# Strassen's seven products in the output stage of a sparse-attention and bilinear feed-forward kernel

## The chip, the cores and the metric

The kernel runs on one core of a Trainium2 chip. The metric is the device time of one execution in microseconds (us), lower is better. Before the change the median was 344.7 us of three runs. An executed program has a span in the profile, from its first to its last instruction, that is about 2 us shorter than the time of the same run. Tile lengths and waits below are parts of a span.

The engines are TensorE (PE; weight loads are PEld), VectorE (DVE), ScalarE (ACT), GpSimd (POOL) and SyncE (SP, whose queue issues transfers and is listed as SPq).

## The reference, cut to what matters

```python
def _attn_ref(q, k, v):                       # 8 batches, 8 heads, 576 tokens, 64 per head
    scores = scale * np.matmul(q, k.transpose(0, 1, 3, 2))
    # heads 0..3: a causal window of 32;  heads 4..7: causal, every 32nd token
    scores = np.where(masks[None], scores, -1e9)
    attn = softmax(scores)                    # written out in the original
    return np.matmul(attn, v)

def _moe_ref(x, w_a, w_b, w_out):             # x: 4608 x 512, w_a and w_b: 512 x 1536, w_out: 1536 x 512
    return (x @ w_a) * (x @ w_b) @ w_out
```

## The kernel before

The 4608 tokens are nine tiles of 512. A tile has 16 slots on TensorE: twelve for the products a and b (one slice of 128 of the 1536 inner columns each, 8 matmuls of 512 columns), then four for the output (12 matmuls each). The attention of the next batches is woven in between the slots. ScalarE copies a out of PSUM, VectorE multiplies it by b, and the product `pf` goes into SBUF as bf16:

```python
def ffn_ab(t, f, mid, ab=None):
    ...
    ab_mm(t, f, ab, range(KD), mid)                       # 2 x 4 matmuls 128x128 by 128x512
    nc.scalar.copy(a_sb, ab[0])
    nc.vector.tensor_mul(pf[:, f, :], a_sb, ab[1])

def ffn_y(t, j, mid):                                     # 128 of the 512 tokens
    ...
        y = psum4["mm"].tile([128, n], F32, ...)          # n = 512 but for the last group
        for f in range(FD):                               # FD = 12
            nc.tensor.matmul(y, lhsT=pf[:, f, 128 * j:128 * (j + 1)], rhs=wo_sb[:, f, c0:c0 + n], ...)
        (nc.scalar.copy if act else nc.vector.tensor_copy)(y_sb, y)
        (nc.scalar if z == 2 else nc.sync).dma_start(out=out[r0:r0 + 128, c0:c0 + n], in_=y_sb)
```

The store is four transfers of 256 KB per tile, whose first dimension is 128 rows of the output. From batch 2 on, the queries and keys of the next batch are transposed by VectorE (`step_D`), and pieces of the result are copied from SBUF to SBUF into `qz` and `kT`, in which the score matmuls (`st`) read them. These copies use the same queue as the stores, SyncE's:

```python
def step_D(b, z, nm, part):
    nc.vector.transpose(t..., src...)
    if last:
        ...
            for e in range(2):                            # both for k and for q
                nc.sync.dma_start(out=dst..., in_=t[64 * c:64 * c + 64, e])            # kT
                for j in range(2):
                    nc.sync.dma_start(out=qz_buf[b % 2][j][z]..., in_=t[r0:r0 + 32, e])  # qz
```

The softmax here doesn't subtract the row's maximum and nothing guards it: scores larger than these inputs give would overflow.

## Time and profile before

| | before |
|---|---|
| time, median of 4 runs | 344.25 us (343.21 to 344.76) |
| span of the profiled run | 341.5 us |
| TensorE busy | 98% of the span |
| granted clock | full in all slices |
| tiles 2, 3, 4, 5 | 35.92, 35.46, 35.45, 35.45 us |
| tiles 6, 7, 8 (to the end of PE) | 34.70, 31.08, 31.30 us |
| after the last matmul | 3.45 us |

Tile lengths are read as the distance from the first a/b matmul of one tile to that of the next. The busy times by stretches are shown in the prediction below. The first is of the kernel before, the stores by their line (columns: line, queue, kind, destination and source, count: shortest, median, longest time to issue one in ns, first and last start).

```profile
L554 SPq DMA_DIRECT2D out_dram<-y_sb x37: 332/338/527, 48.8 to 337.8; - x37
...
DMA to landing us min/median/max: 1.6/2.2/5.9
```

At the median a store of 256 KB holds the queue for 0.34 us. The second is the order of time on SyncE's queue, at the start of tile 3 (start, duration, queue, line, what, count).

```profile
132.41 3.13 SPq L554 DMA_DIRECT2D out_dram<-y_sb  x2
140.98 0.55 SPq L302 DMA_DIRECT2D qz00s<-tq  x1
141.58 0.58 SPq L302 DMA_DIRECT2D qz01s<-tq  x1
```

The last two stores of tile 2 (a row that names several issues spans from the first to the end of the last, with gaps) are out at 135.5 us. VectorE has transposed q at 141; the copies of q follow without a gap, about 0.6 us each. The fourth of these copies is in the chain of waits, with the time from its issue to its landing:

```profile
142.84 3.64 DMA qz01s<-tq
```

The score matmuls start as it lands, at 146.52, so this time has little slack. Even so, in the view of waits, all that TensorE waited for copies of q over the span is three waits of 1.2, 0.7 and 0.5 us.

### The profile page before, as it was taken

What the parts mean: (1) busy time and instruction counts of PE and PEld (TensorE: products, weight loads), DVE (VectorE), ACT (ScalarE), POOL (GpSimd) and SP (SyncE); (2) the same over time, 40 slices, a digit from 0 to 9 for tenths busy, and PEclk for the clock granted to TensorE, in tenths of its full rate; (3) what the DMA queues carried; (4) which work ended last, traced back from release to release, by engine and by line L of the source; (5) the groups of instructions that cost most, each with busy time, mean ns of one, the idle gap of its engine ahead of it and who ended that gap; (6) DMA issues with size and microseconds to landing.
All of it is one profiled execution on the core that took longest, in us unless ns stands there. A gap on an engine that the chain in (4) does not pass through costs nothing.

```text
span 341.5 us, 6887 instructions
## 1 busy us (share of the span) xinstructions
PE 333.1 (98%) x2520; PEld 173.7 (51%) x2520; DVE 205.1 (60%) x400; ACT 203.9 (60%) x331; POOL 140.4 (41%) x247
## 2 busy tenths in 40 slices
PE   8999999989989999999999999999999999999995
PEld 6754555445545555555555555555555444444444
DVE  6866657758759766876578846885666333303331
ACT  5754865368767765876587657775688533223311
POOL 8945539898537434653465346633000000000000
PEclk9999999999999999999999999999999999999999
DMA  9999999997999599969997989888220110021002
GB/s 160 154 203 197 202 176 172 179 154 89 129 200 101 90 99 185 99 110 91 165 104 133 77 168 96 132 80 145 76 59 2 61 63 0 0 92 34 0 31 94
DMA packets 102242, 37.56 MB, mean 110 GB/s; under 512 B 77632, under 2 KB 97728, under 8 KB 102208
## 3 DMA queue, kind: packets, MB, share of 16 engines
q0 software_dynamic: 87760, 19.58, 63.7%
q1 hardware_dynamic: 14304, 17.47, 16.2%
q8 instruction: 20, 0.33, 0.4%
q14 instruction: 14, 0.11, 0.1%
q10 hardware_dynamic: 144, 0.07, 0.1%
HBM read 39.71 MB, written 9.44 MB: 144 GB/s over the span
## 4 chain that ended last, share of the span: by engine, by line
PE 70%; DMA 17%; SPq 3%; DVE 3%; ACT 3%; POOL 2%; issue 2%; DVEq 0%; ACTq 0%
PE mm L518 41%; PE mm L546 20%; DMA vl<-in_v_dram 4%; PE o L438 3%; PE st L340 3%; DMA k<-in_k_dram 3%; DMA wa_sb<-in_moe_w_a_dram 3%; SPq L302 2%; DMA qz01l<-tq 2%; PE misc L153 2%; DMA out_dram<-y_sb 1%; DMA qz01s<-tq 1%; ACT xr L447 1%; DMA qz11s<-tq 1%; DVE tq L283 1%
## 5 line engine op out<-in xcount | busy, mean ns | idle before, releaser
L518 PE MATMUL mm<-xT,wb_sb 128*128 128x512 bf16 x424 | 110.1, 379 | 0.3
L518 PE MATMUL mm<-xT,wa_sb 128*128 128x512 bf16 x424 | 110.2, 379 | 0.1
L536 DVE TENSOR_TENSOR pf<-a_sb,mm 128x512 bf16<-128x512 f32 x106 | 71.9, 678 | 48.3 <-PE mm L518 25.5
L546 PE MATMUL mm<-wo_sb,pf 128*128 128x512 bf16 (+2 forms) x456 | 99.6, 368 | 0.1
L535 ACT COPY a_sb<-mm 128x512 f32<-128x512 f32 x106 | 62.1, 586 | 45.4 <-PE mm L518 43.0
L518 PEld LDWEIGHTS <-wb_sb 128*128 128x128 bf16 x432 | 41.7, 98 | 49.5 <-issue 1.3
L546 PEld LDWEIGHTS <-pf 128*128 128x128 bf16 x456 | 41.5, 98 | 42.3 <-issue 0.4
L518 PEld LDWEIGHTS <-wa_sb 128*128 128x128 bf16 x432 | 38.1, 98 | 34.2 <-issue 0.2
L552 ACT COPY y_sb<-mm 128x512 f32<-128x512 f32 (+2 forms) x35 | 20.0, 571 | 46.6 <-PE mm L546 38.6
L348 ACT ACTIVATE p<-st 128x576 bf16<-128x576 f32 (+1 forms) x64 | 41.7, 651 | 8.8 <-PE st L340 8.2
L447 ACT ACTIVATE xr<-o 64x576 f32<-64x576 f32 x48 | 31.1, 647 | 23.5 <-PE o L438 23.3
L454 DVE TENSOR_TENSOR xT<-o,xr 64x288 bf16<-64x288 f32 x48 | 21.6, 450 | 33.1 <-ACT xr L448 32.8
L448 ACT ACTIVATE xr<-xr 64x576 f32<-64x576 f32 x48 | 32.8, 682 | 1.5
L452 DVE TENSOR_TENSOR xT<-o,xr 64x288 bf16<-64x288 f32 x48 | 21.6, 450 | 16.9 <-ACT xr L448 16.4
L678 POOL CAST pace<-pf 1x1 f32<-1x1 bf16 x51 | 11.6, 227 | 41.5 <-DVE pf L536 41.3
L358 DVE TENSOR_TENSOR p<-p,mask_l 128x576 int16<-128x576 int16 x32 | 14.6, 455 | 17.1 <-ACT p L348 17.1
L218 POOL DMA_DIRECT2D vs<-in_v_dram x24 | 19.6, 817 | 9.9 <-issue 9.9
L194 POOL DMA_DIRECT2D kl<-in_k_dram x24 | 16.0, 666 | 6.7 <-issue 5.0
L194 POOL DMA_DIRECT2D ql<-in_q_dram x24 | 16.0, 666 | 6.6 <-DMA wo_sb<-in_moe_w_out_dram 3.8
L185 POOL DMA_DIRECT2D natk<-in_k_dram x24 | 14.6, 610 | 3.6 <-issue 3.0
L185 POOL DMA_DIRECT2D natq<-in_q_dram x24 | 14.6, 609 | 0.0
L678 POOL COPY pace<-y_sb 1x1 f32<-1x1 f32 x22 | 4.2, 189 | 24.2 <-ACT y_sb L552 24.2
(116 smaller groups left out, 316.2 us busy)
## 6 DMA issues: line engine op xcount, KB each, us to landing
out_dram<-y_sb SPq DMA_DIRECT2D x35, 256.0 KB, 2.4
vl<-in_v_dram POOLq DMA_DIRECT2D x7, 384.0 KB, 6.6
kl<-in_k_dram POOLq DMA_DIRECT2D x24, 72.0 KB, 2.8
ql<-in_q_dram POOLq DMA_DIRECT2D x24, 72.0 KB, 3.3
vs<-in_v_dram POOLq DMA_DIRECT2D x24, 72.0 KB, 3.6
wo_sb<-in_moe_w_out_dram POOLq DMA_DIRECT2D x4, 384.0 KB, 11.9
natk<-in_k_dram POOLq DMA_DIRECT2D x20, 72.0 KB, 3.3
natq<-in_q_dram POOLq DMA_DIRECT2D x20, 72.0 KB, 3.3
```

The lines of the kernel that those rows point to most:

```text
L185: nc.gpsimd.dma_start(out=t[32 * h:32 * h + n], in_=bass.AP(tensor=src.tensor, offset=(b * H + HL + h) * S * D, ap=[[RS * D, n], [YS * RS ...
L194: nc.gpsimd.dma_start(out=t[32 * h:32 * h + 32], in_=src[b, h].rearrange("(i y) d -> y i d", y=32))
L348: nc.scalar.activation(p[:M, :, :W], st[:M, :, :W], ACT.Exp, scale=scale)
L447: nc.scalar.activation(r, sums, ACT.Ln)
L448: nc.scalar.activation(r, r, ACT.Exp, scale=-1.0)
L452: nc.vector.tensor_mul(dst[:, W * half:W * (half + 1)], o[:64, j, :W], r[:, j])
L454: nc.vector.tensor_mul(dst.rearrange("d (p r) -> d p r", r=RS)[:, :, G * half:G * (half + 1)], o[:64, j, :W].rearrange("d (g p) -> d p g", ...
L518: nc.tensor.matmul(ps_, lhsT=w[:, kk, 128 * f:128 * (f + 1)], rhs=xT[:, kk, TTOK * t:TTOK * (t + 1)], start=(kk == first), stop=(kk == last))
L535: nc.scalar.copy(a_sb, ab[0])
L536: nc.vector.tensor_mul(pf[:, f, :], a_sb, ab[1])
L546: nc.tensor.matmul(y, lhsT=pf[:, f, 128 * j:128 * (j + 1)], rhs=wo_sb[:, f, c0:c0 + n], start=(f == 0), stop=(f == FD - 1))
L552: (nc.scalar.copy if act else nc.vector.tensor_copy)(y_sb, y)
```

## The change

An output tile is seen as a 2 by 2 block product: the tokens in two halves, the inner dimension in even and odd slices, the output columns in two halves of 256. Strassen's scheme, in the form with few additions, makes this from seven products in place of eight. TensorE is what the kernel is bound by, so one eighth of the output matmuls is to be saved, at the price of additions on engines that have time.

- TensorE: 84 matmuls of 256 columns per tile in place of 48 of 512, for tiles 2 to 8, in an order of products that frees banks early ("3417526", in the last tile "3412567").
- VectorE: nine sums of `pf` per tile, ten sums of the weights once (in the slots of tile 2), four additions that read PSUM.
- GpSimd: the last two subtractions per tile.
- ScalarE: three copies out of PSUM in place of four.
- The tokens of one half aren't neighbours. They alternate with the other half in runs of 16, so `pf` is written in that order, and the store is taken apart again: eight stores of 128 KB per tile, each of which writes 8 runs of 16 rows.
- Room for this: xT holds four batches in place of eight (which cuts tile 4's matmuls in two halves), some loads share a buffer with the sums, and a fourth bank joins the rotation of `mm`.

```diff
@@ ffn_ab @@
-        nc.vector.tensor_mul(pf[:, f, :], a_sb, ab[1])
+        if t in FAST_Y:                                    # tiles 2 to 8
+            halves = lambda x: x.rearrange("p (a i s) -> p a i s", i=2, s=16)
+            nc.vector.tensor_mul(pf[:, f, :].rearrange("p (i a s) -> p a i s", i=2, s=16), halves(a_sb), halves(ab[1]))
+        else: ...
@@ the sums @@
+    def fast_w(n, gs):   # five sums of quarters of the weights, two pieces each
+        nc.vector.tensor_tensor(wf[:, n, gs], a[:, gs], b[:, gs], op=op)
+    def fast_s(t, n, gs):   # sums of quarters of pf
+        if n == 0:   nc.vector.tensor_tensor(s[:, :, 0:HT], x[:, :, 0, 0], x[:, :, 1, 1], op=ALU.add)
+        elif n == 1: ...                                   # 1024 elements
+        else: ...                                          # 1024 elements
@@ the output, y_plan @@
+        def store(y, i, j, q=slice(0, 2), n=slice(0, HN)):
+            rows = out[TTOK * t:TTOK * (t + 1), HN * j:HN * (j + 1)].rearrange("(q a i s) c -> a s i q c", q=2, i=2, s=16)
+            for z in range(q.start, q.stop):
+                nc.sync.dma_start(out=rows[:, :, i, z, n], in_=y[:, z, n])
+        def post(k): ...                 # what follows each product; among others:
+                    nc.gpsimd.tensor_tensor(v["y11"], v["e"], v["y12"], op=ALU.subtract)
+                    store(v["y11"], 0, 0)
+        for k in "3412567" if tail else "3417526":
+            ...
+                    for g in range(FG):                    # 6
+                        nc.tensor.matmul(dst, lhsT=lhs(g, q), rhs=rhs(g)[:, n], ...)
@@ the schedule @@
+        for n in range(5):
+            for z in range(2):
+                do(32 + 2 * n + z, fast_w, n, slice(3 * z, 3 * z + 3))      # slots of tile 2
+        for t in FAST_Y: ...             # fast_s in slots 3 to 11 of each tile
```

Cut: the ring of xT, the shared buffer, `mm_bank`, most of `post`, and the special last product of tile 8.

More of the change, by code (lines that the diff above doesn't have):

```diff
@@ L26 @@
 WCH = (0, 2, 5, 8, 10, 12)
+FAST_Y = (2, 3, 4, 5, 6, 7, 8)
 @with_exitstack
@@ L156 @@
     cur = {}
-    xT = const.tile([128, KD, n_tok], BF16)
+    XR = 4
+    xT = const.tile([128, KD, XR * S], BF16)
     wa_sb = wp.tile([128, KD, d_ff], BF16)
@@ L160 @@
     wo_sb = wp.tile([128, FD, d_model], BF16)
+    FG = FD // 2
+    HT = TTOK // 2
+    HN = d_model // 2
+    wf = wp.tile([128, 5, FG, HN], BF16, name="wf")
+    wov = wo_sb.rearrange("p (g e) (j n) -> p e j g n", e=2, j=2)
+    def fast_w(n, gs):
+        a, b, op = ((wov[:, 0, 1], wov[:, 1, 1], ALU.subtract), (wov[:, 1, 0], wov[:, 0, 0], ALU.subtract),
+                    (wov[:, 0, 0], wov[:, 1, 1], ALU.add), (wov[:, 0, 0], wov[:, 0, 1], ALU.add),
+                    (wov[:, 1, 0], wov[:, 1, 1], ALU.add))[n]
+        nc.vector.tensor_tensor(wf[:, n, gs], a[:, gs], b[:, gs], op=op)
     tl = {}
@@ L168 @@
     nats = {}
+    shared = {}
     def load_qk(b, strided, heads=range(HL), names="kq"):
@@ L174, in load_qk @@
                 n, R, h0 = (NP, RS, HL) if strided else (96, RL, 0)
-                if (b, nm, strided) not in nats:
-                    nats[b, nm, strided] = nat.tile([n, HL, R, D], BF16, tag=f"{nm}{R}", name=f"{nm}{R}", bufs=1)
-                t = nats[b, nm, strided]
+                w0 = {"k6": 0, "q6": 1536, "k8": 3072, "q8": 5120}[f"{nm}{R}"]
+                if b not in shared:
+                    shared[b] = nat.tile([128, 5 * FD * TTOK // 4], BF16, tag="shared", name="shared")
+                t = nats[b, nm, strided] = shared[b][:n, w0:w0 + HL * R * D].rearrange("p (h r d) -> p h r d", r=R, d=D)
                 hs = slice(heads[0], heads[-1] + 1)
@@ L449, in step_VT @@
         for j in range(2):
-            dst = xT[64 * j:64 * j + 64, c, S * b:S * (b + 1)]
+            dst = xT[64 * j:64 * j + 64, c, S * (b % XR):S * (b % XR + 1)]
             if c < 2:
@@ L469, in X_e @@
         tv = tp.rearrange("d (g p) -> d g p", p=n)
-        dst = xT[:, c, S * b:S * (b + 1)]
+        dst = xT[:, c, S * (b % XR):S * (b % XR + 1)]
         if c >= 2:
@@ L511, with mm_bank @@
     pfs = {}
+    used = [0]
+    def mm_bank(shape):
+        nm = "tp" if used[0] % 4 == 3 and used[0] >= 0 else "mm"
+        used[0] += 1
+        return psum4[nm].tile(shape, F32, tag=nm, name="mm")
     def ab_mm(t, f, ab, kks, mid=None, first=0, last=KD - 1):
+        n = min(TTOK, XR * S - TTOK * t % (XR * S))
+        cuts = [(0, n)] + ([(n, TTOK - n)] if n < TTOK else [])
         for w, ps_ in zip((wa_sb, wb_sb), ab):
@@ L517, in ab_mm @@
             for kk in kks:
-                nc.tensor.matmul(ps_, lhsT=w[:, kk, 128 * f:128 * (f + 1)], rhs=xT[:, kk, TTOK * t:TTOK * (t + 1)],
-                                 start=(kk == first), stop=(kk == last))
+                for c0, n in cuts:
+                    x0 = (TTOK * t + c0) % (XR * S)
+                    nc.tensor.matmul(ps_[:, c0:c0 + n], lhsT=w[:, kk, 128 * f:128 * (f + 1)], rhs=xT[:, kk, x0:x0 + n],
+                                     start=(kk == first and c0 == 0), stop=(kk == last and c0 == cuts[-1][0]))
     def ffn_ab(t, f, mid, ab=None):
@@ L525, in ffn_ab @@
         if ab is None:
-            ab = [psum4["mm"].tile([128, TTOK], F32, tag="mm", name="mm") for _ in range(2)]
+            ab = [mm_bank([128, TTOK]) for _ in range(2)]
             if f == 0:
@@ L535, in ffn_ab @@
         nc.scalar.copy(a_sb, ab[0])
-        nc.vector.tensor_mul(pf[:, f, :], a_sb, ab[1])
-        return pf[:1, f, :1]
+        if t in FAST_Y:
+            halves = lambda x: x.rearrange("p (a i s) -> p a i s", i=2, s=16)
+            nc.vector.tensor_mul(pf[:, f, :].rearrange("p (i a s) -> p a i s", i=2, s=16), halves(a_sb), halves(ab[1]))
+        else:
+            nc.vector.tensor_mul(pf[:, f, :], a_sb, ab[1])
+        return pf[:1, f, :1]
+    pss = {}
+    def fast_s(t, n, gs):
+        if t not in pss:
+            pss[t] = nat.tile([128, 5 * FD * TTOK // 4], BF16, tag="shared", name="ps").rearrange("p (g m) -> p g m", g=FG)
+        s = pss[t][:, gs]
+        x = pfs[t].rearrange("p (g e) (i m) -> p g e i m", e=2, i=2)[:, gs]
+        if n == 0:
+            nc.vector.tensor_tensor(s[:, :, 0:HT], x[:, :, 0, 0], x[:, :, 1, 1], op=ALU.add)
+        elif n == 1:
+            nc.vector.tensor_tensor(s[:, :, HT:3 * HT].rearrange("p g (i m) -> p g i m", i=2), x[:, :, 0], x[:, :, 1], op=ALU.add)
+        else:
+            nc.vector.tensor_tensor(s[:, :, 3 * HT:].rearrange("p g (e m) -> p g e m", e=2), x[:, :, :, 1], x[:, :, :, 0],
+                                    op=ALU.subtract)
@@ new lines, with y_plan, f32t, post @@
+    yst = {}
+    def y_plan(t):
+        pf, s = pfs[t], pss[t]
+        full = lambda e, i: (lambda g, q: pf[:, 2 * g + e, HT * i + 128 * q:HT * i + 128 * (q + 1)])
+        summed = lambda n: (lambda g, q: s[:, g, HT * n + 128 * q:HT * n + 128 * (q + 1)])
+        wsum = lambda n: (lambda g: wf[:, n, g])
+        wfull = lambda e, j: (lambda g: wov[:, e, j, g])
+        bank = {}
+        v = {}
+        def f32t(nm, bufs):
+            return fsb.tile([128, 2, HN], F32, tag=nm, name=nm, bufs=bufs)
+        def store(y, i, j, q=slice(0, 2), n=slice(0, HN)):
+            rows = out[TTOK * t:TTOK * (t + 1), HN * j:HN * (j + 1)].rearrange("(q a i s) c -> a s i q c", q=2, i=2, s=16)
+            for z in range(q.start, q.stop):
+                nc.sync.dma_start(out=rows[:, :, i, z, n], in_=y[:, z, n])
+        def post(k):
+            if k == "3":
+                v["a"] = f32t("ya", 1)
+                nc.scalar.copy(v["a"], bank["a"])
+            elif k == "4":
+                v["w"] = v["a"]
+                nc.vector.tensor_tensor(v["w"], bank["b"], v["a"], op=ALU.add)
+            elif k == "1":
+                v["e"] = f32t("ye", 1)
+                nc.vector.tensor_tensor(v["e"], bank["c"], v["w"], op=ALU.add)
+            elif k == "7":
+                nc.vector.tensor_tensor(v["e"], v["e"], bank["d"], op=ALU.subtract)
+            elif k == "2":
+                v["y21"] = f32t("y_sb", 4)
+                nc.scalar.copy(v["y21"], bank["b"])
+                store(v["y21"], 1, 0)
+                if tail:
+                    nc.gpsimd.tensor_tensor(v["w"], v["w"], v["y21"], op=ALU.subtract)
+            elif k == "5":
+                v["y12"] = f32t("y_sb", 4)
+                nc.scalar.copy(v["y12"], bank["a"])
+                store(v["y12"], 0, 1)
+                if tail:
+                    nc.gpsimd.tensor_tensor(v["e"], v["e"], v["y12"], op=ALU.subtract)
+                else:
+                    v["y11"] = f32t("y_sb", 4)
+                    nc.gpsimd.tensor_tensor(v["y11"], v["e"], v["y12"], op=ALU.subtract)
+                    store(v["y11"], 0, 0)
+            else:
+                v["y22"] = f32t("y_sb", 4)
+                if tail:
+                    nc.vector.tensor_tensor(v["y22"], bank["c"], v["w"], op=ALU.add)
+                else:
+                    nc.vector.tensor_tensor(v["w"], bank["c"], v["w"], op=ALU.add)
+                    nc.gpsimd.tensor_tensor(v["y22"], v["w"], v["y21"], op=ALU.subtract)
+                store(v["y22"], 1, 1)
+        def y11(d, q=slice(0, 2), n=slice(0, HN)):
+            if "y11" not in v:
+                v["y11"] = f32t("y_sb", 4)
+            nc.vector.tensor_tensor(v["y11"][:, q, n], v["e"][:, q, n], d, op=ALU.subtract)
+            store(v["y11"], 0, 0, q, n)
+        tail = t == NT - 1
+        plan = {"3": ("a", full(0, 0), wsum(0)), "4": ("b", full(1, 1), wsum(1)), "1": ("c", summed(0), wsum(2)),
+                "2": ("b", summed(2), wfull(0, 0)), "5": ("a", summed(1), wfull(1, 1)), "6": ("c", summed(3), wsum(3)),
+                "7": ("d", summed(4), wsum(4))}
+        for k in "3412567" if tail else "3417526":
+            b, lhs, rhs = plan[k]
+            new = b not in bank
+            if new and not (tail and k == "7"):
+                bank[b] = mm_bank([128, 2, HN])
+            for q in range(2):
+                cuts = (slice(0, HN),)
+                if tail and k == "7":
+                    if q == 1:
+                        cuts = (slice(0, 128), slice(128, HN))
+                        end = psum4["o"].tile([128, 2, 512], F32, tag="o", name="end")
+                    else:
+                        end = mm_bank([128, 1, 512])
+                for z, n in enumerate(cuts):
+                    dst = end[:, z, :n.stop - n.start] if tail and k == "7" else bank[b][:, q, n]
+                    for g in range(FG):
+                        nc.tensor.matmul(dst, lhsT=lhs(g, q), rhs=rhs(g)[:, n], start=g == 0 and (tail and k == "7" or new and q == 0),
+                                         stop=g == FG - 1, skip_group_check=True)
+                        if g == FG - 1:
+                            if tail and k == "7":
+                                y11(dst.unsqueeze(1), slice(q, q + 1), n)
+                            elif q == 1:
+                                post(k)
+                        yield v
@@ L539, in ffn_y, with ffn_ys @@
+    def ffn_ys(t, j, mid):
+        if j == 0:
+            yst[t] = y_plan(t)
+        n = 21 + (6 if (t, j) == (NT - 1, 3) else 0)
+        for i in range(n):
+            v = next(yst[t])
+            if i == n // 2:
+                mid()
+        if j == 3:
+            for _ in yst[t]:
+                pass
+        return v[("a", "e", "e", "w")[j]][:1, 0, :1]
     def ffn_y(t, j, mid):
@@ L543, in ffn_y @@
         for z, n in enumerate((256, 128, 128) if (t, j) == (NT - 1, 3) else (d_model,)):
-            y = psum4["mm"].tile([128, n], F32, tag="mm", name="mm")
+            y = mm_bank([128, n])
             for f in range(FD):
@@ L549, in ffn_y @@
                     mid()
-            y_sb = fsb.tile([128, n], F32, tag="y_sb", name="y_sb", bufs=3)
+            y_sb = fsb.tile([128, n], F32, tag="y_sb", name="y_sb", bufs=4)
             act = t < NT - 1 or (j + z) % 2 == 1
@@ L631 @@
         for t in range(NT):
-            slots += [(ffn_ab, t, f) for f in range(FD)] + [(ffn_y, t, j) for j in range(4)]
+            slots += [(ffn_ab, t, f) for f in range(FD)] + [(ffn_ys if t in FAST_Y else ffn_y, t, j) for j in range(4)]
         steps = {}
@@ L672 @@
             do(i, fill_v, t)
+        for n in range(5):
+            for z in range(2):
+                do(32 + 2 * n + z, fast_w, n, slice(3 * z, 3 * z + 3))
+        for t in FAST_Y:
+            for n, at_ in ((0, (3, 7, 11)), (2, (4, 8, 11)), (1, (5, 9, 11))):
+                for z in range(3):
+                    do(16 * t + at_[z], fast_s, t, n, slice(2 * z, 2 * z + 2))
         for i, (fn, t, j) in enumerate(slots):
+            if i == 0:
+                used[0] = -1000 * 3
+            elif i == 16:
+                used[0] = 0
             mid = lambda: take(i - 0.5)
-            done = fn(t, j, mid) if fn is ffn_y else fn(t, j, mid, first.get(j) if t == 0 else None)
+            done = fn(t, j, mid) if fn is not ffn_ab else fn(t, j, mid, first.get(j) if t == 0 else None)
             if i > 13 and i in at:
```

## The prediction

> **What bounds the kernel now.** I read the page first (busy shares, the chain that ended last), then busy time by stretches cut at the token tiles, then the groups of instructions, then the order of time around one tile and around the end. The page's first part:
>
> ```profile
> PE 333.1 (98%) x2520; PEld 173.7 (51%) x2520; DVE 205.1 (60%) x400; ACT 203.9 (60%) x331; POOL 140.4 (41%) x247
> ```
>
> TensorE is busy in 98% of the span, at full granted clock in every slice, and the chain that ended last is 70% TensorE, 41% of it the a/b products and 20% the output products (the line that the change rewrites). Busy time by stretches shows that this holds within each tile (columns: window, length, then busy us and instructions of each engine, clock, DMA share, GB/s). The windows are tiles 2, 3, 4, 5, 6, 7 and 8:
>
> ```profile
> 98.60:134.50 35.90, 35.74 (x260) 18.27 (x258) 26.65 (x49) 25.01 (x41) 18.07 (x35) 1.00 0.91 127
> 134.50:170.00 35.50, 35.42 (x262) 18.32 (x259) 24.79 (x46) 24.91 (x40) 17.94 (x35) 1.00 0.91 119
> 170.00:205.50 35.50, 35.47 (x262) 18.29 (x259) 24.80 (x46) 24.91 (x40) 18.01 (x35) 1.00 0.92 119
> 205.50:241.00 35.50, 35.46 (x262) 18.34 (x259) 24.80 (x46) 24.96 (x41) 16.58 (x33) 1.00 0.92 119
> 241.00:275.80 34.80, 34.80 (x249) 17.76 (x246) 19.24 (x37) 24.32 (x39) 0.44 (x2) 1.00 0.14 45
> 275.80:306.90 31.10, 31.10 (x146) 14.07 (x144) 8.25 (x12) 9.38 (x16) 0.00 (x0) 1.00 0.09 34
> 306.90:338.00 31.10, 31.10 (x169) 15.33 (x166) 9.92 (x15) 8.58 (x15) 0.00 (x0) 1.00 0.10 35
> ```
>
> The reader should see two things: PE (first pair) fills every one of these tiles, so a matmul less is time less; and VectorE (third pair) has 24.8 of 35.5 us in tiles 3 to 5, 26.65 in tile 2, but 8 to 10 in tiles 7 and 8. So the room for more VectorE work is about 10 us in an attention tile and 20 us after the attention.
>
> **What one output matmul costs, and one of half its width.** The mean durations in the groups (379 ns for 512 columns) include [...]overlap; the pitch has to come from the order of time. In tile 7, 48 matmuls took 10.36 us in the chain, 0.216 us each. The half width is there too, because the last output group of tile 8 is split 256, 128, 128. From the order of time at the end:
>
> ```profile
> 335.44 0.69 DVE L552 COPY y_sb<-mm 128x512 f32<-128x512 f32 x1 [4.49 <-DMA out_dram<-y_sb]
> 336.75 0.37 ACT L552 COPY y_sb<-mm 128x256 f32<-128x256 f32 x1 [3.31 <-PE mm L546]
> 337.48 0.29 DVE L552 COPY y_sb<-mm 128x128 f32<-128x128 f32 x1 [1.35 <-PE mm L546]
> 338.27 0.27 ACT L552 COPY y_sb<-mm 128x128 f32<-128x128 f32 x1 [1.15 <-DMA out_dram<-y_sb]
> ```
>
> Each copy starts when its group of 12 matmuls is done: 336.75 - 335.44 = 1.31 us for 12 matmuls of 256 columns, 0.109 each; 0.73 to 0.79 for 12 of 128, about 0.063 each. Each loads its own weights (98 ns as recorded, overlapping), so doubling the number of weight loads does not show at 256 columns.
>
> [...]The mask product (two 16-bit operands, 576 elements) took 455 ns[...], and the fp32 product of 512 took up to 689[...].
>
> **The change, part by part.**
>
> *TensorE.* An output tile was 48 matmuls of 512 columns, 10.36 us. It becomes 7 products of 12 matmuls of 256: 84 x 0.1092 = 9.17 us, 1.19 us less. Six tiles (2 to 7) give 7.1 us. In tile 8 the old 10.58 us becomes 78 x 0.109 + 12 x 0.063 = 9.26, 1.32 less. Sum 8.5 us, 2.4% of 344.7: the ceiling. The ring of four batches for xT splits tile 4's a/b matmuls in two halves of 256: 192 x 0.109 against 20.7 us, under 0.3 us. A fourth bank for "mm" lets TensorE run further ahead, but it is not waiting now.
>
> *VectorE, sums of pf.* Per tile three pieces each of 512, 1024 and 1024 bf16 elements. From the mask product, which starts the next instruction 0.37 us later (duration 0.455 less about 0.08 of overlap), I scale: 0.34 us for 512, 0.60 for 1024; 3 x 1.54 = 4.6 us.
>
> *VectorE, evacuation.* Four PSUM additions per tile at 0.61 to 0.69 us: 2.6 us. ScalarE copies three banks in place of four: 0.59 us less, no matter. So VectorE in tiles 3 to 5 goes from 24.8 to about 32.0 us, while TensorE goes to 34.3.
>
> *VectorE, sums of the weights.* Ten of 768 bf16 elements, all in slots of tile 2, 0.47 us each: 4.7 us. Tile 2: 26.65 + 4.6 + 2.6 + 4.7 = 38.6 us of VectorE work, against 34.7 of TensorE.
>
> *GpSimd.* Two subtractions a tile[...]; with 18 of 35 us busy there is room[...].
>
> *Stores.* Eight of 128 KB per tile in place of four of 256, at 0.34 us of queue time each; off the path until the end.
>
> **Where VectorE stops lying beside.** Per pair of a/b slots (3.97 us of TensorE) VectorE has two products (1.22), two writes of xT (0.92), a mask (0.37) and a transposition (0.70): 3.2 us, 0.77 free. In slots 3 to 5 and 7 to 9 the sums add 1.54 per three slots where 1.15 is free: it lags by 0.4 to 0.9 us and recovers. The first products need pf of the tenth f-slice 0.55 us after the output begins (was 2.2), the eleventh at 1.85, and product 1 needs its last sum at 3.3 us, against 2.9 without lag. So a lag over 0.4 us costs TensorE the rest: I charge 0.3 us to each of tiles 3, 4 and 5, 0.9 in all. In tile 2 the overload is 38.6 - 34.7 = 3.9 us; about 1 us can be carried in the four banks and the o banks, so I charge 3 us. Tiles 6, 7 and 8 have little VectorE work and keep all. At the end, the last stores go one behind another on one queue, whereas before the last one went by ScalarE's: 0.5 us. Sum: 8.5 - 3.0 - 0.9 - 0.5 - 0.2 (split tile) = 3.9 us; 344.7 - 3.9 = 340.8.
>
> **The rivals.** (a) *VectorE keeps up everywhere*, because waits in its queue (48 us before pf, 50 before xT over the span) are idle time that is simply filled: then 8.5 - 0.7 = 7.8 us, 337 us. For it: 10 us free in tiles 3 to 5, a fourth bank; against it: the sum for tile 2 exceeds TensorE's time with no wait counted. (b) *VectorE becomes the bound in all attention tiles*: [...]pf slower because it is written in runs of 16, waits on ScalarE[...]. At 36 to 37 us per tile in 2 to 5 that is 344 to 348. For it: 93% load[...]. Against it: the order of its instructions lets pf and xT pass between the sums. (c) *The transfer of the transposed q becomes the wait.* In the order of time the transposition in slot 1 of a tile is followed by ten issues of about 0.6 us, and the score matmuls of slot 5 start as their piece lands (a chain piece "DMA qz01s<-tq" of 3.64 us ends at the start of "PE st" in tile 3): there is no slack, so VectorE's lag at the start of a tile is paid there. Adding durations in its order after the output stage, VectorE's first pf lands 2.9 us after TensorE has ended it, where it was 3.3, so I expect no more than the same[...].
>
> **Range and chances.** The ceiling (344.7 - 8.5 = 336.2) is barely below the 2% line (337.8), and passing that needs 81% of the gain kept, in spite of tile 2: 0.13. Slower by 2% needs 15 us of new stalls, 3 us in each attention tile: 0.06. The rest, 0.81. Eight times in ten between 337.0 (rival a) and 345.5 (b or c).
>
> **What would show each step.** Tiles 7 and 8 should each be 1.2 us shorter, 84 matmuls at 0.109 us: if not, the width costs more than the tail showed. The groups should show sums of pf at about 0.42 and 0.69 us and of weights at 0.56[...]. In the stretches, tile 2 should be 37 to 38 us with VectorE over 95% busy and TensorE idle 2 to 4 us, waiting for pf or banks; tiles 3 to 5 34.5 to 35 us, VectorE near 32. If tile 2 has no TensorE idle, (a) is right; if tiles 3 to 5 show idle before the score matmuls put down to a DMA, (c).[...]

## The result

The changed kernel takes 353.65 us (350.67 to 356.05, four runs, one of them, 356.05, slow) against 344.25 (343.21 to 344.76). Executions over 1.5% slower than the fastest of the same kernel are left out of the means. All ratios in this document are the mean time of one kernel's fast runs over that of the other's fast runs of the same rounds, so they are not quite the ratios of the medians quoted. Here it is 1.025, with a 95% interval of 1.0202 to 1.0298: slower by over 2%, outside the predicted range, and at odds with the most likely of the three outcomes.

The page of the changed kernel says at once that TensorE is no longer full. These are the engines' totals and two rows of the 40 slices (tenths busy, and granted clock):

```profile
PE 326.5 (93%) x2818; PEld 206.4 (59%) x2850; DVE 258.1 (73%) x500; ACT 200.7 (57%) x325; POOL 170.8 (49%) x287
...
PE   9999999999799889979996999599999999999992
...
PEclk9999999999999999999999999989999999999998
```

Its busy time fell from 333.1 to 326.5 us, as it was meant to, while the span grew from 341.5 to 351.4. A slice is 8.8 us here. The holes of 7, 6 and 5 tenths begin at 149, 184 and 220 us, 7 to 12 us into the tiles 3, 4 and 5. The busy time by stretches gives it by tile (columns as in the prediction; the windows are tiles 2, 3, 4, 5, 6, 7 and 8 of the changed kernel):

```profile
99.69:137.60 37.91, 34.98 (x288) 21.38 (x292) 36.53 (x71) 24.63 (x41) 18.69 (x37) 1.00 0.74 90
137.60:174.60 37.00, 34.30 (x288) 21.37 (x291) 31.42 (x59) 24.28 (x39) 20.59 (x38) 1.00 0.89 113
174.60:212.19 37.59, 34.67 (x394) 31.23 (x392) 32.12 (x61) 24.32 (x40) 21.11 (x40) 1.00 0.89 113
212.19:251.77 39.58, 35.82 (x289) 22.28 (x293) 32.00 (x60) 24.30 (x40) 20.89 (x38) 0.96 0.84 107
251.77:285.07 33.30, 33.14 (x277) 21.12 (x280) 26.73 (x51) 23.84 (x38) 7.67 (x11) 1.00 0.18 50
285.07:314.96 29.89, 29.79 (x181) 17.60 (x181) 15.89 (x25) 8.79 (x15) 5.78 (x10) 1.00 0.13 38
314.96:345.60 30.64, 30.10 (x186) 17.71 (x185) 16.47 (x27) 8.78 (x15) 6.93 (x10) 1.00 0.15 46
```

Tiles 6, 7 and 8, which have little or no attention left in them, are shorter than before. In tiles 2 to 5 TensorE has 2.7 to 3.8 us of idle time each, where it had at most 0.2. In tile 2 VectorE explains it: 36.5 of 37.9 us busy. In tiles 3 to 5 VectorE has 5.5 to 7.6 us to spare and is not the bound, which stores_late below shows.

The next table sets the tiles side by side. The column "predicted" is the length before with the prediction's own charges for that tile; the last two columns are experiments that are told below.

| us | before | predicted | after | plain_8 | plain_w_early_end |
|---|---|---|---|---|---|
| start of tile 2 | 98.69 | 98.7 | 99.69 | 98.87 | 100.11 |
| tile 2 | 35.92 | 37.7 | 37.91 | 37.91 | 34.67 |
| tile 3 | 35.46 | 34.6 | 37.01 | 34.19 | 33.82 |
| tile 4 | 35.45 | 34.8 | 37.58 | 34.50 | 34.60 |
| tile 5 | 35.45 | 34.6 | 39.58 | 34.31 | 34.32 |
| tile 6 | 34.70 | 33.5 | 33.30 | 33.30 | 33.30 |
| tile 7 | 31.08 | 29.9 | 29.89 | 29.89 | 29.89 |
| tile 8, to the end of PE | 31.30 | 30.0 | 30.67 | 30.6 | 30.1 |
| after it | 3.45 | 3.9 | 5.8 | 3.6 | 4.0 |
| span | 341.5 | 337.6 | 351.4 | 337.2 | 334.7 |

The differences from before to after are +1.0 (the start, which varies by that and more from run to run in these experiments), +2.0, +1.55, +2.1, +4.1, -1.4, -1.2, -0.6 and +2.3, in all +9.9 us. Against the prediction, nearly all is in tiles 3 to 5 (10.2 us) and in the end (1.9 us).

What TensorE waited for is in the view of waits of the changed kernel (engine, tile and line, what it waited for: us in all, times, longest):

```profile
PE st L356 <- DMA qz01s<-tq: 6.0, 3, 3.1
PE st L356 <- DMA qz11s<-tq: 3.2, 2, 2.9
```

These are the score matmuls that wait for copies of q, 9.2 us with these two rows. A third row (qz11l, 2.3 us) is not special to the changed kernel: there is one of 1.2 us before. The copies use the same queue as the stores, SyncE's. SyncE's queue in tiles 3 and 4 in order of time:

```profile
136.32 6.37 SPq L603 DMA_DIRECT2D out_dram<-y_sb  x8
143.75 0.60 SPq L318 DMA_DIRECT2D qz00s<-tq  x1
...
173.55 7.33 SPq L603 DMA_DIRECT2D out_dram<-y_sb  x8
181.00 0.90 SPq L318 DMA_DIRECT2D qz10s<-tq  x1
181.94 1.03 SPq L318 DMA_DIRECT2D qz11s<-tq  x1
183.02 1.47 SPq L318 DMA_DIRECT2D qz10s<-tq  x1
```

The eight stores of a tile now come bunched at the start of the next one and hold the queue for 6.4 and 7.3 us. The copies of q begin behind them: in tile 3 one microsecond after the queue is free, in tile 4 straight on. That is not later than before: the first copy is issued 6.15, 6.39 and 6.15 us into tiles 3, 4 and 5, where it was 6.37 in each. Some of the copies take longer to issue (0.6 to 1.0 us in place of 0.55 to 0.6; the 1.47 of tile 4 doesn't count, since plain_8 and stores_late below have 1.4 in the same place). What grew most is the time from a copy's issue to its landing. Two pieces of the chain show it, one of a store in tile 3 and one of the fourth copy in tile 5 (the fourth copy of tile 3 took 3.64 us before):

```profile
141.18 8.18 DMA out_dram<-y_sb
```

```profile
221.05 6.41 DMA qz01s<-tq
```

The views give no landings for the stores of this kernel, but they can be counted from the semaphore records of the kept trace: on each of SyncE's eight DMA semaphores the recorded updates are 16 for every other transfer and 9 for each of these stores, without a rest. By this count the last store lands 11.8, 12.5 and 12.6 us into tiles 3, 4 and 5 (2.8 before), no copy lands before it, and the first four copies land 4.9 to 7.3 us after their issue (2.2 to 3.6 before). The last of the four is there 14.1, 14.8 and 15.3 us into the tile in place of 11.7 to 11.9, and the score matmuls start then. Why a copy lands late behind unfinished stores isn't shown.

The chain view must be read with care here. For tile 3 it names another copy, issued at 149.38 when the store of 141.18 had landed, as what the score matmuls at 151.62 waited for. By the count that copy landed at 153.71, after they had started. They wait for several semaphores, and the view puts that down to the last update of any of them; the third and fourth copy, which landed at 151.49 and 151.69, fit.

By the stores' line:

```profile
L603 SPq DMA_DIRECT2D out_dram<-y_sb x57: 603/603/2057, 136.3 to 347.3; - x57
```

The median issue is 0.60 us for half of the bytes that took 0.34 before. So the loss was seen quickly to sit in the copies of q, behind the stores. What these views cannot tell is why: because there are twice as many stores; because their rows are interleaved; because VectorE or GpSimd delays them until they come bunched; or because too much else is on the way.

Tile 5 lost more than its neighbours. Two stretches of it, cut where the idle time ends:

```profile
219.50:228.50 9.00, 5.40 (x41) 2.74 (x41) 3.88 (x8) 4.29 (x7) 2.98 (x8) 1.00 1.06 155
228.50:236.80 8.30, 8.25 (x50) 3.98 (x49) 7.72 (x15) 5.02 (x9) 4.73 (x8) 0.79 0.35 58
```

In the first, TensorE is idle for 3.6 of 9 us; in the second it is busy throughout, at a granted clock of 0.79. An estimate of what this cost is 8.25 x 0.21 = 1.7 us. The lower clock follows an idle stretch here; that the one caused the other was not tested by itself.

### The profile page after: what moved, and what is told of

The parts are those of the page before. It is cut to its first block, busy times and chain, and to the rows that moved or that the text cites. A ratio compares the mean times of both kernels' runs of the same rounds, so it can differ in the third digit from the quotient of the medians.

```text
span 351.4 us, 7721 instructions
## 1 busy us (share of the span) xinstructions
PE 326.5 (93%) x2818; PEld 206.4 (59%) x2850; DVE 258.1 (73%) x500; ACT 200.7 (57%) x325; POOL 170.8 (49%) x287
## 4 chain that ended last, share of the span: by engine, by line
PE 54%; DMA 22%; POOL 8%; DVE 7%; issue 4%; SPq 3%; ACT 0%; DVEq 0%; POOLq 0%
PE mm L545 31%; PE mm L668 15%; DMA vl<-in_v_dram 6%; DMA out_dram<-y_sb 4%; DMA shared<-in_k_dram 3%; DMA wa_sb<-in_moe_w_a_dram 3%; PE st L356 3%; PE o L454 2%; DMA qz01s<-tq 2%; SPq L318 2%; PE misc L154 2%; DMA qz11s<-tq 1%; DVE pf L565 1%; POOL natk L201 1%; DVE xT L470 1%
## 5 line engine op out<-in xcount | busy, mean ns | idle before, releaser
L545 PE MATMUL mm<-xT,wb_sb 128*128 128x512 bf16 (+1 forms) x465 | 109.7, 359 | 0.9 <-DVE pf L565 0.7
L545 PE MATMUL mm<-xT,wa_sb 128*128 128x512 bf16 (+1 forms) x451 | 108.3, 358 | 1.0
L545 PEld LDWEIGHTS <-wb_sb 128*128 128x128 bf16 x480 | 46.5, 98 | 45.9 <-issue 2.6
L840 POOL CAST pace<-pf 1x1 f32<-1x1 bf16 x77 | 23.2, 302 | 98.1 <-DVE pf L565 97.5
L668 PEld LDWEIGHTS <-ps 128*128 128x128 bf16 x426 | 40.7, 98 | 5.1 <-issue 0.6
L668 PE MATMUL mm<-wf,ps 128*128 128x256 bf16 x246 | 29.1, 273 | 0.0
L697 PE MATMUL mm<-wo_sb,pf 128*128 128x512 bf16 x93 | 22.9, 379 | 0.7 <-DMA wo_sb<-in_moe_w_out_dram 0.5
L668 PE MATMUL mm<-wf,pf 128*128 128x256 bf16 x168 | 21.0, 273 | 1.0 <-DVE pf L565 0.9
L668 PE MATMUL mm<-wo_sb,ps 128*128 128x256 bf16 x168 | 21.0, 273 | 0.0
L567 DVE TENSOR_TENSOR pf<-a_sb,mm 128x512 bf16<-128x512 f32 x22 | 14.8, 674 | 7.6 <-ACT a_sb L562 5.7
L299 DVE STREAM_TRANSPOSE tk<-kl 128x576 bf16<-128x576 bf16 x12 | 9.1, 768 | 12.1 <-DMA natk<-in_k_dram 5.1
```

Source lines behind the costliest of these rows:

```text
L545: nc.tensor.matmul(ps_[:, c0:c0 + n], lhsT=w[:, kk, 128 * f:128 * (f + 1)], rhs=xT[:, kk, x0:x0 + n], start=(kk == first and c0 == 0), sto ...
L668: nc.tensor.matmul(dst, lhsT=lhs(g, q), rhs=rhs(g)[:, n], start=g == 0 and (tail and k == "7" or new and q == 0), stop=g == FG - 1, skip_g ...
L840: nc.gpsimd.tensor_copy(pace, done)
```

## The experiments

Ten kernels ran, all with correct outputs, all of their timed runs compared with the kernel before in the same rounds on the same chip. Before the first of them I had these theories. The first (theory 1 in the expectations) is that the stores on SyncE's queue hold up the copies of q, by their number or by their shape. Its rivals were that VectorE's added work makes the copies late (rival b and c of the prediction), that the lower clock is the loss and not its result, and that GpSimd's subtractions are to blame (theory 4), since the masks of the local heads take VectorE 531 ns at the mean in the changed kernel, where they took 455, and the last two outputs come late.

### stores_late: the stores of a tile are issued after the copies of q

```diff
+    late = []
+    def flush():
+        while late:
+            late.pop(0)()
         def store(...):
-            for z in range(q.start, q.stop):
-                nc.sync.dma_start(out=rows[:, :, i, z, n], in_=y[:, z, n])
+            def go(): ...                    # the same two lines
+            if t < 6: late.append(go)
+            else: go()
+        for t in FAST_Y:
+            if t < 6: do(16 * (t + 1) + 2, flush)
```

> The eight output stores of tiles 2 to 5 are queued on SyncE only after the ten copies of the transposed q of the next tile's first slots; nothing else differs from the changed kernel. Theory 1 (the stores, bunched in front of those copies on the same queue, delay the score matmuls): TensorE's idle time before the score matmuls put down to the qz copies, 9 us in the changed kernel from tile 2 on, goes to under 1.5 us; tiles 3, 4 and 5 come to 34.3 to 35 us each (37.0, 37.6, 39.6 now), the drop of the granted clock in tile 5 goes away, and the time is 343 to 346 us. Theory 2 (VectorE at 32 us of work per tile is the bound): tiles 3 to 5 stay at 36 us or more, the time above 350. Theory 3 (the 16 DMA engines are full, order does not matter): waits move to other copies, 348 to 351.

Measured: 341.43 us against 344.36, ratio 0.9915 (0.9865 to 0.9965), some 2 us better than theory 1 had it. Nothing but the place of the stores on the queue changed. SyncE's order of time in tile 3, the last copy of q and then the stores:

```profile
149.20 0.59 SPq L318 DMA_DIRECT2D qz01s<-tq  x1
149.89 6.31 SPq L609 DMA_DIRECT2D out_dram<-y_sb  x8
```

The stores are as slow to issue as in the changed kernel, but there is nothing behind them for which TensorE waits. The first copy is issued 6.4 us into each of tiles 3 to 5, hardly other than there, but the first four land 2.3 to 4.0 us after their issue. Tiles 3 to 5 took 34.22, 34.59 and 34.02 us in place of 37.01, 37.58 and 39.58, and TensorE's waits for q in these tiles fell to 0.2 us. The mean granted clock of this run was 0.998, where it was 0.991. So the stores in front of the copies are the loss in tiles 3 to 5, the lower clock in tile 5 goes with them, and VectorE's work, which is the same here, is not it. Tile 2 stayed at 37.91.

### tiles_6_to_8: the seven products only where there is no more attention to prepare

```diff
-FAST_Y = (2, 3, 4, 5, 6, 7, 8)
+FAST_Y = (6, 7, 8)
-                do(32 + 2 * n + z, fast_w, n, slice(3 * z, 3 * z + 3))
+                do(96 + 2 * n + z, fast_w, n, slice(3 * z, 3 * z + 3))
```

> Seven products only in tiles 6, 7 and 8, after which no scores follow; the sums of the weights move to tile 6. All theories agree that TensorE's gain remains: tiles 6, 7 and 8 at 33.4, 29.9 and 30.5 us (34.7, 31.1, 31.1 before), tiles 2 to 5 as before at 35.5, and the end 2 us longer than before. 342 to 343 us, 0.4 to 0.7% faster than before. If the time is above 345, something outside the output stage (ring for xT, shared load tile, fourth bank) costs time, which theory 1 denies.

Measured: 344.22 us against 344.36, ratio 1.0 (0.9941 to 1.0059). This missed the 342 to 343 that I expected. The tiles did what they should: tiles 2 to 5 are as before (35.27 to 35.77), tiles 6 to 8 took 34.16, 29.89 and 30.67, together 2.4 us less. It was given back at the two ends: 0.8 us up to tile 6, which is the start (of the size of its variation), and 1.9 us after the last matmul, 5.4 us in place of 3.45. So the end of the changed kernel costs 2 us whatever happens in the middle.

### plain_halves: the halves as plain blocks of tokens, four stores of 256 KB

The first half is now tokens 0 to 255 of the tile, the second 256 to 511; one store has 128 partitions by 2 rows.

```diff
-            halves = lambda x: x.rearrange("p (a i s) -> p a i s", i=2, s=16)
-            nc.vector.tensor_mul(pf[:, f, :].rearrange("p (i a s) -> p a i s", i=2, s=16), halves(a_sb), halves(ab[1]))
+            nc.vector.tensor_mul(pf[:, f, :], a_sb, ab[1])
-            rows = out[...].rearrange("(q a i s) c -> a s i q c", q=2, i=2, s=16)
-            for z in range(q.start, q.stop):
-                nc.sync.dma_start(out=rows[:, :, i, z, n], in_=y[:, z, n])
+            rows = out[...].rearrange("(i q p) c -> p i q c", i=2, q=2)
+            nc.sync.dma_start(out=rows[:, i, q, n], in_=y[:, q, n])
```

> The two token halves are plain halves in place of runs of 16, so each quarter of an output tile goes out in one store of 256 KB rather than two of 128 KB, with the same rows of 1 KB: four stores per tile. Theory 1 in the form 'SyncE's issue time of 8 x 0.6 to 0.9 us is what delays': issue time per tile falls from 6.4-7.3 us to under 3, waits for the qz copies fall by half or more, time 347 to 350. Theory 1 in the form 'the bytes in front must drain first': the same megabyte stands in front, landing stays at 7 to 8 us, waits stay within 2 us of the 9, time 351 to 354.

Measured: 340.23 us against 344.36, ratio 0.9873 (0.9817 to 0.993). The expectation was 347 us at best, so I was wrong about the size in either form in which I then held theory 1: I took the interleaving for a small part. A store's issue is 0.378 us at the median and it lands after 2.9; tiles 3 to 5 took 34.35, 35.04 and 34.03 us. Two things changed at once, number and shape; plain_8 parts them.

### subs_on_vector: the last subtractions on VectorE, the stores as they were

```diff
-                    nc.gpsimd.tensor_tensor(v["y11"], v["e"], v["y12"], op=ALU.subtract)
+                    nc.vector.tensor_tensor(v["y11"], v["e"], v["y12"], op=ALU.subtract)
```
(and the same for the other three subtractions)

> The last two subtractions of each tile go back from GpSimd to VectorE. Theory 1: VectorE has 1.3 us more per tile, masks fall from 0.53 to 0.46 us, the last stores are ready 0.6 us earlier, and the waits for the qz copies stay: within 2 us of the changed kernel. Theory 2 (VectorE the bound): 1.3 us longer in each of tiles 2 to 5, 358 us or more. Theory 4 (the stores wait for GpSimd, and that delays the qz copies): waits for the qz copies fall by over 3 us, time 349 to 351.

Measured: 349.71 us against 344.36, ratio 1.0149 (1.0099 to 1.02). It is quicker than the changed kernel (ratio 1.025, measured in other rounds), with waits for q of 6.2 us in tiles 3 to 5 where they were 8.9, and a tile 5 of 37.89 us in place of 39.58. This is the time of theory 4, though the waits fell by 2.7 us and not by over 3; it fits as a part of the loss. The mask products of the local heads fell from 531 ns at the mean to 451 at the median (446 to 460). The slow stores were still there (eight took 6.5 us of the queue in tile 3), and most of the loss with them.

### plain_8: plain halves, but eight stores of 128 KB

```diff
             (pf and rows as in plain_halves)
             for z in range(q.start, q.stop):
-                nc.sync.dma_start(out=rows[:, :, i, z, n], in_=y[:, z, n])
+                nc.sync.dma_start(out=rows[:, i, z, n], in_=y[:, z, n])
```

> As plain_halves (340.2 us), but each quarter of an output again goes out in two stores of 128 KB, eight per tile as in the changed kernel: only the interleaving of the rows in runs of 16 differs from the changed kernel. Theory A (what made the stores slow is their shape: 8 runs of 16 rows in place of 128 equal steps): issue time near 0.35 us each, landing near 3 us, time 339 to 342. Theory B (what made them slow is their number and size): issue 0.6 us each, waits for the qz copies back to 6 us or more, time 349 to 354.

Measured: 339.03 us against 343.58, ratio 0.9865 (0.9827 to 0.9904). This kernel has the same number of stores of the same size at the same places as the changed one. It differs only in which rows make up a store, and in the order in which `pf` is written (the product that writes it takes VectorE 681 ns at the mean, 682 in the changed kernel). The stores by their line:

```profile
L602 SPq DMA_DIRECT2D out_dram<-y_sb x57: 332/430/1562, 135.5 to 334.4; - x57
...
DMA to landing us min/median/max: 1.6/2.6/4.0
```

and tiles 3 to 5 by stretches:

```profile
136.78:170.97 34.19, 33.83 (x289) 21.61 (x292) 31.66 (x59) 24.30 (x39) 20.69 (x38) 1.00 0.96 124
170.97:205.47 34.50, 34.45 (x393) 31.20 (x392) 32.07 (x61) 24.34 (x40) 21.07 (x40) 1.00 0.97 124
205.47:239.78 34.31, 33.98 (x288) 21.71 (x292) 31.99 (x60) 24.32 (x40) 20.74 (x38) 1.00 0.97 123
```

TensorE is nearly full again, with VectorE's busy time (32 us) and GpSimd's (21 us) as they were in the changed kernel. The eight stores of tile 2 held the queue for 4.8 us, not 6.4, were out 2.6 us before the copies of q began and had landed 0.1 us after that; the copies then took 0.55 to 0.59 us each to issue and the first four landed 2.5 to 3.8 us after it (all this in tile 3). The end was 3.6 us. So the number of stores is not the cause (four stores gave 0.9873, eight 0.9865), their interleaved rows are. The end's extra 2 us came from the same source. The interval lies below 1 and above 0.98: faster than the kernel before, but by less than 2%.

### plain_w_early: plain_halves with the sums of the weights in slots 19 to 23

In this run and the next, the sums of the weights were moved out of tile 2 into tile 1.

```diff
-                do(32 + 2 * n + z, fast_w, n, slice(3 * z, 3 * z + 3))
+                do(19 + n, fast_w, n, slice(3 * z, 3 * z + 3))
```

> plain_halves with the ten sums of the weights moved from the slots of tile 2 to slots 19 to 23 of tile 1, where no transposition stands. Theory of the prediction (tile 2 is bound by VectorE because of them): tile 2 falls from 37.9 to 34.5-35.5 us, tile 1 grows by less than 0.5, the time is 2.0 to 3.2 us below plain_halves: 337 to 338.5. Rival (VectorE is full in tile 1 too, or tile 2 is held by the sums of pf): tile 2 and 1 together lose less than 1 us.

Measured: 337.82 us (335.88 to 340.31) against 343.58, ratio 0.9826 (0.9768 to 0.9884). Tile 2 fell from 37.91 to 34.28 us. The profiled run was the slowest of the four; its tile 1 took 43.69 us, at a granted clock of 0.92 and with waits for copies of q of up to 1.9 us, where most others took 38.8 to 39.7. That isn't the price of the moved sums: the next kernel has them in tile 1 too, which took 39.68 us there, at full clock. So 3.6 us in tile 2 are shown. The ratio is better than those of plain_halves and plain_8 by 0.004 to 0.005, some 1.5 us, which is less than half of that; the spread of the start is as large as what is missing.

### plain_w_early_end: the same, with the last stores on two queues and a bank of its own for the last piece

```diff
-            nc.sync.dma_start(out=rows[:, i, q, n], in_=y[:, q, n])
+            (nc.scalar if tail and i == j == 1 else nc.sync).dma_start(out=rows[:, i, q, n], in_=y[:, q, n])
+                        end2 = mm_bank([128, 1, 512])
-                    dst = end[:, z, ...] ...
+                    dst = (end2[:, 0] if z == 1 else end[:, 0])[...] ...
```

> The same, with the last two groups of the end in two tiles of PSUM, so that TensorE doesn't wait 0.43 us for VectorE before the last six matmuls, and one store of the end on ScalarE's queue. 0.4 to 0.9 us below plain_w_early. Below 0.2 us: the end is set by the landing of the last store alone.

Measured: 337.47 us (336.47 to 339.03) against 343.58, ratio 0.9816 (0.9769 to 0.9863). It beats both kernels; whether by 2% is open, since the interval holds 0.98. Beside plain_w_early it is 0.35 us better, just short of the expected 0.4 to 0.9 and within the spread, so the edit of the end isn't shown to help: in the profiled run TensorE ended tile 8 in 30.1 us in place of 30.7, but the time after it grew from 3.4 to 4.0. It was made because of a wait in the changed kernel's end: the last six matmuls wait 0.43 us for VectorE to read the bank that holds the piece before. Tile 2 of this kernel:

```profile
100.11:134.78 34.67, 33.98 (x288) 21.70 (x292) 32.42 (x61) 24.65 (x41) 18.49 (x36) 1.00 0.86 106
```

VectorE has 32.4 us in place of 36.5, and TensorE's idle time in tile 2 is 0.7 us in place of 2.9. The prediction's account of tile 2 stands: VectorE was over what fits.

### plain_subs_vector: plain_halves with the last subtractions on VectorE

```diff
             (pf, rows and stores as in plain_halves)
-                    nc.gpsimd.tensor_tensor(v["y11"], v["e"], v["y12"], op=ALU.subtract)
+                    nc.vector.tensor_tensor(v["y11"], v["e"], v["y12"], op=ALU.subtract)
             (and the same for the other three subtractions)
```

> plain_halves with the last two subtractions of each tile on VectorE. In the changed kernel this took 4 us off; if that was because the stores came earlier and stood less in the way of the qz copies, then with the cheap stores nothing of it remains, and VectorE's 1.3 us more per tile (less 0.5 for masks[...]) cost 0 to 2 us: 340 to 342.5. If GpSimd's subtractions hurt by themselves[...], 337 to 339.5.

Measured: 339.40 us (337.98 to 341.55) against 343.58, ratio 0.9854 (0.9806 to 0.9902). plain_8, with them on GpSimd, had 0.9865 in the same rounds, and plain_halves 0.9873 in others: no difference within the spread. (By its number alone, 339.40 lies in the range of the second theory, that the subtractions hurt by themselves; but plain_8, which has them on GpSimd, took 339.03 in the same rounds.) So with cheap stores it isn't shown to matter where the subtractions are. The 4 us that they gave in subs_on_vector were seen only beside slow stores. A likely reason is that outputs that come sooner move the stores forward on the queue: in tile 4 the last store was out 5.1 us into the tile in place of 6.3, and landed at 11.3 in place of 12.5. This is argued, and no run takes it apart.

### before_in_runs: the kernel before, with stores of 8 runs of 16 rows

```diff
-        nc.vector.tensor_mul(pf[:, f, :], a_sb, ab[1])
+        if t > 1: ...                        # pf in runs of 16, as in the changed kernel
-            (...).dma_start(out=out[r0:r0 + 128, c0:c0 + n], in_=y_sb)
+            if t > 1:
+                rows = out[...].rearrange("(q a i s) c -> a s i q c", q=2, i=2, s=16)
+                dst = rows[:, :, j // 2, j % 2]
+            (...).dma_start(out=dst, in_=y_sb)
```

> The kernel before, with 48 matmuls per output tile and its four stores of 256 KB spread over the output stage, but from tile 2 on pf is written, and the rows are stored, in the changed kernel's runs of 16: the shape alone, without seven products, sums or bunching. If the shape makes a store slow by itself: issue time rises from 0.34 to 0.6 us or more and landing from 2.2 us to over 3.5; TensorE pays only what reaches the qz copies of slot 1, 0 to 3 us in all: 344 to 347. If the shape is slow only together with the bunching: issue and landing as before, 343 to 344.5.

Measured: 347.96 us (346.45 to 350.58) against 343.73, ratio 1.0157 (1.0099 to 1.0215). Here is no Strassen at all, only the shape of the store, and it costs some 4 us, one more than the top of what I had expected. The interval lies above 1, but whether it is 2% is open. The issue time is that of the changed kernel for twice the bytes:

```profile
L562 SPq DMA_DIRECT2D out_dram<-y_sb x37: 333/604/747, 48.9 to 338.4; - x37
```

In the profiled run, the fastest of the four, the attention tiles stayed near those of before (tile 5 36.16 us, the others within 0.1). Four stores, spread over the output stage, were out in time: SyncE had issued them by 135.5 us, five before the copies of q. The loss was mostly at the end, where ScalarE's last copy waited 3.3 us for a store that had not landed, to get its buffer. So slow stores alone do not stop the score matmuls; they have to be still on the way when the copies come, as the bunched eight are. Four slow stores bunched like that, or eight spread out, were not tried.

### runs_of_64: the changed kernel, with runs of 64 tokens in place of 16

```diff
-  ... i=2, s=16 ...
+  ... i=2, s=64 ...                          # in the three places
```

A store then writes 2 runs of 64 rows: fewer, longer pieces of the output.

> The changed kernel with rows interleaved in runs of 64 in place of 16, so that a store is 2 runs of 64 rows rather than 8 of 16. If any shape of three dimensions is slow: issue 0.6 us, landing 7 us, 350 to 355 us as the changed kernel. If it is the short runs: between the changed kernel and the plain one, 340 to 349, with issue under 0.6 us.

Measured: 447.53 us (447.06 to 449.29) against 343.73, ratio 1.304 (1.2998 to 1.3082). Neither expectation was near: if length of the runs were what matters, 64 would be the better. The stores by their line:

```profile
L603 SPq DMA_DIRECT2D out_dram<-y_sb x57: 503/2578/4613, 134.5 to 435.9; - x57
```

The median issue is 2.6 us, tiles 3 to 5 took about 60 us each, and the score matmuls waited up to 23 us at a time for copies of q. At the median the issue of 128 KB took 0.43 us in plain rows (plain_8, 0.33 at the least), 0.60 in 8 runs of 16 (0.60 at the least) and 2.58 in 2 runs of 64 (0.50 at the least, so the shape alone does not need the rest). So 2 runs were worse than 8; the number and the length of the runs change together here, and no run parts them.

The traces don't say how the work of one transfer is divided, but the updates that they record on its semaphore differ by shape: 16 for a store of plain rows, 9 for 8 runs, 3 for 2 runs, in each case counted over all of SyncE's DMA semaphores without a rest. With runs, one update comes 0.4 us after the end of each issue and the others, 8 and 2, from 1.8 us on; with plain rows all 16 come from 1.0 us on. The mean busy share of the DMA engines differs too, where only stores are on the way. First the changed kernel (285 to 300 us), then plain_8 (273 to 288), then runs_of_64 (353 to 395), each in 40 slices, tenths of the time of the 16 engines that the view counts:

```profile
DMA  2553455555555555541000000000000000000000
```

```profile
DMA  7628000877887600000000000000000000000000
```

```profile
DMA  0000000000211111111111111111111000000011
```

With 8 runs the share stops at 0.5, with plain rows it reaches 0.8, with 2 runs it stays at 0.1. An estimate from these shares is that about 8, 13 and 2 of the 16 were busy at a time. The same answers give the rates: mostly 140 to 194 GB/s in the first, 230 to 292 in the full slices of the second, 47 to 49 in most slices of the third. Why the shape has this effect isn't shown.

## Why the prediction was wrong

**The step that failed** is this one: "*Stores.* Eight of 128 KB per tile in place of four of 256, at 0.34 us of queue time each; off the path until the end." Its term was 0.5 us, all at the end. In place of it the runs showed 0.60 us at the median and up to 2.06 for an issue, a landing of 8.2 us for one store, and a place on the path in three tiles, since the copies of q behind them landed 4.9 to 7.3 us after their issue and not 2.2 to 3.6: plain_8, with plain rows, shortened tiles 3 to 5 by 2.8, 3.1 and 5.3 us and the end by 2.2, in all 13.4 us. (The medians differ by 14.6 us, in different rounds.) The duration of 0.34 was taken from a store with another shape, as if bytes alone set it. That the shape had changed is in the diff, in one line of `rearrange`.

**One look would have shown where to ask.** The order of the changed kernel's instructions on SyncE, which could be had before the run, has a tile's stores ahead of the ten copies of q and k of the next. What the new shape costs was in no trace of the kernel before, whose stores were of plain rows.

**Rival (c) had the right wait and the wrong cause.** It named the copies of q as having no slack, which was so, and said that VectorE's lag would be paid there, with 345.5 us as the upper end of the range. The transposition was on time: the copies started at 143.75 us, 6.2 us into tile 3, and 6.4 us into it before. What was late was their landing. It also said that idle time before the score matmuls, put down to a DMA, would show it, which it did.

**What held.** TensorE's 84 matmuls of 256 columns took what was predicted from the tail of the kernel before, 9.17 us; a piece of the chain of the changed kernel, in tile 7, is shown below. One reading of that tail was off: the prediction has each copy start when its group of matmuls is done, but the last row of its lines says that this copy waited for a store. So the 0.79 us are not 12 matmuls of 128 columns; their starts in the trace are 0.056 us apart, not 0.063, which is 0.1 us in tile 8.

```profile
305.95 9.17 PE mm L668 x84
```

Tile 7 was 1.2 us shorter as predicted. The sums cost about what was predicted, here the groups of VectorE by form (line, engine, operation, tiles, shapes, count | busy us, mean ns | idle before):

```profile
L582 DVE TENSOR_TENSOR ps<-pf 128x1024 bf16<-128x1024 bf16 x21 | 14.4, 686 | 0.2
L578 DVE TENSOR_TENSOR ps<-pf 128x512 bf16<-128x512 bf16 x21 | 8.4, 400 | 0.2
L174 DVE TENSOR_TENSOR wf<-wo_sb 128x768 bf16<-128x768 bf16 x10 | 5.3, 532 | 0.1
```

0.69, 0.40 and 0.53 us stand against 0.69, 0.42 and 0.56, although the operands have large strides between their rows. An estimate from two durations of the kernel before, 455 ns for a mask product of 576 16-bit elements and 689 ns for an fp32 product of 512, gives the same three figures if an fp32 element counts as two of 16 bits. Tile 2 lost to VectorE what was charged (37.91 us where 37.7 was predicted, VectorE 96% busy), and plain_w_early_end showed that moving the weight sums gives it back. The size of this charge is in part luck: VectorE's work in tile 2 was put at 38.6 us and measured 36.5, and of the overload 1 us was to be carried in the banks. With plain stores tiles 3 to 5 took 34.2 to 34.5 us where 34.5 to 35 was predicted, so the charge of 0.3 us for VectorE's lag was, if anything, too high. Rivals (a) and (b) fell: VectorE did not keep up in tile 2, and it was not the bound in tiles 3 to 5.

**GpSimd's subtractions** took 1.28 and 1.31 us at the mean in the groups of the changed kernel, and those at its end 1.27. A mask product beside one took longer. In the order of time of plain_8, a mask product at 135.64 us, which began inside a subtraction, took 1.09 us, and the next, at 137.85, 0.43:

```profile
135.12 1.28 POOL L630 TENSOR_TENSOR y_sb<-ye,y_sb 128x512 f32<-128x512 f32 x1
135.64 1.09 DVE L374 TENSOR_TENSOR p<-p,mask_l 128x576 int16<-128x576 int16 x1
```

In the changed kernel there is one such mask in each of tiles 2 to 5's output stages, 1.09 to 1.10 us long, some 0.64 us more than the 0.45 of the others; and in plain_subs_vector, which has no subtraction on GpSimd, the time is the same within the spread.

**Without the slow stores the gain was put too low, but near.** It was predicted as 3.9 us; plain_8 gained 4.55 (339.03 against 343.58 in the same rounds). So the rest of the sum held.

**What stays open.** Why the changed kernel loses more in tile 5 (4.1 us) than in tiles 3 and 4 is shown in part by the lower clock, which came with the idle time and went with it; the order of cause was not tested. Why the subtractions on VectorE gain 4 us beside slow stores is argued only. Tile 2 starts 97.9 to 101.1 us into the span in eleven of the twelve profiled runs, and at 104.1 in one; why is open. And why the copies land late while slow stores are unfinished is not shown: no run takes it apart. Nor was it tried whether the same stores on another queue would do the same.

## What to carry to other kernels

The cost of a transfer comes from its shape, not from its bytes alone: here 128 KB took 0.43, 0.60 or 2.58 us of the queue at the median by the order of its rows. When a change gives a store another order of rows, time it anew, and take no duration from a store of another shape. When a change adds transfers, go through the queue that issues them and ask what stands behind them and when TensorE needs that; look at when it lands, and not only at when it is issued. Where an instruction waits for several semaphores, check that the transfer which the view names had landed by then. A change that saves the bound engine's time can be right in all of its arithmetic and still lose to one line that only brings its results out; here the same seven products with plain rows are 1.4% faster than the kernel before (1.0 to 1.7 by the interval), and with the sums of weights moved to an emptier tile and a changed end 1.8% (1.4 to 2.3).
